# Transposing q and k on VectorE, with SBUF-to-SBUF moves, in place of TensorE transposes

## The chip, the cores and the metric

One Trainium2 chip (trn2), one core of it. The metric is the device time of one execution in microseconds (us), the median of the runs given. Times compared here are of fast runs. "The granted clock" is the share of full TensorE speed that the throttle granted, as the profile records it.

## The reference

Eight batches of strided sparse attention, whose output feeds a bilinear FFN. Four of the eight heads are *local* (each query sees the 32 positions up to itself), four are *strided* (it sees the earlier positions with the same remainder modulo 32).

```python
B, H, S, D = 8, 8, 576, 64
scores = (1/sqrt(D)) * q @ k.transpose(0, 1, 3, 2)
rel = pos[:, None] - pos[None, :]
mask_local   = (rel >= 0) & (rel < 32)                           # heads 0..3
mask_strided = (rel >= 0) & (pos[None, :] % 32 == pos[:, None] % 32)  # heads 4..7
attn_out = softmax(where(mask, scores, -1e9)) @ v
x = attn_out.transpose(0, 2, 1, 3).reshape(B * S, H * D)         # 4608 tokens x 512
out = ((x @ w_a) * (x @ w_b)) @ w_out                            # 512 -> 1536 -> 512
```

## The kernel before

The FFN runs in nine tiles of 512 tokens; each tile is 16 slots (12 of products with w_a and w_b, 4 of products with w_out). Batch 0's attention comes first; that of batch *b* is then woven into the slots of the tiles before it is needed. Its score matmuls on TensorE (PE) take q and k with the head dimension on the partitions; the program makes that layout with transposes on PE as well, and copies bring the result out of PSUM. `L` numbers in the profile lines are lines of the kernel file.

```python
def load_qk(b, strided):
    n, R, h0 = (NP, RS, HL) if strided else (96, RL, 0)
    for nm, src in (("q", q), ("k", k)):
        t = nat.tile([n, HL, R, D], BF16, tag=f"{nm}{R}", name=f"{nm}{R}")
        nc.gpsimd.dma_start(out=t, in_=src[b, h0:h0 + HL].rearrange("h (p r) d -> p h r d", r=R))
...
def step_T(b, c, nm):                       # transposes of one head pair on PE
    ...
        for g in range(8):                  # strided: 8 of 72 columns; local: 6 of 96
            nc.tensor.transpose(tv[:, g, :], sv[:, ...], ident[:NP, :NP])
    if nm == "k":
        nc.vector.tensor_copy(perm(kT_buf[b % 2][:, c, PAD:]), tv)
    else:                                   # each head's half of the rows, the rest stays zero
        for j in range(2):
            pr = slice(64 * j, 64 * j + 64)
            nc.scalar.copy(perm(qz_buf[b % 2][j][pr, c, :]), tv[pr])
...
def ffn_ab(t, f):
    ...                                     # 4 matmuls with w_a, 4 with w_b, into PSUM "mm" (3 buffers)
    nc.scalar.copy(a_sb, ab[0])
    nc.vector.tensor_mul(pf[:, f, :], a_sb, ab[1])      # called pf below
...
with tc.manual_schedule(engines={ENG.PE, ENG.SP, ENG.Pool}):   # in program order; VectorE's and
    ...                                                        # ScalarE's order is the compiler's
```

The softmax here doesn't subtract the row's maximum and nothing guards it: scores larger than these inputs give would overflow.

## Time and profile before

| | before |
|---|---|
| median of 3 runs | 365.77 us (364.46 to 365.85) |
| span of the profiled execution | 364.4 us |
| PE busy / granted clock | 343.3 us (94%), 2785 matmuls / 1.00 |
| VectorE (DVE) busy | 188.1 us (52%) |
| first FFN matmul | 29.5 us |
| the nine tiles | 46.4, 38.1, 37.0, 37.0, 37.0, 37.0, 36.5, 31.1, 34.8 us |

The last row is how the whole text reads time: a tile's length is the distance from its first w_a matmul to that of the next tile (to the span's end for the last). Here PE is the bound (94% busy, 91% of the chain that ended last), so a tile that is longer than its PE work has a wait in it. The profile's lines are shown in the prediction below.

### The profile page before, as it was taken

What the parts mean: (1) busy time and instruction counts of PE and PEld (TensorE: products, weight loads), DVE (VectorE), ACT (ScalarE), POOL (GpSimd) and SP (SyncE); (2) the same over time, 40 slices, a digit from 0 to 9 for tenths busy, and PEclk for the clock granted to TensorE, in tenths of its full rate; (3) what the DMA queues carried; (4) which work ended last, traced back from release to release, by engine and by line L of the source; (5) the groups of instructions that cost most, each with busy time, mean ns of one, the idle gap of its engine ahead of it and who ended that gap; (6) DMA issues with size and microseconds to landing.
All of it is one profiled execution on the core that took longest, in us unless ns stands there. A gap on an engine that the chain in (4) does not pass through costs nothing.

```text
span 364.4 us, 6796 instructions
## 1 busy us (share of the span) xinstructions
PE 343.3 (94%) x2785; PEld 185.5 (51%) x2785; DVE 188.1 (52%) x369; ACT 163.3 (45%) x268; POOL 90.8 (25%) x108
## 2 busy tenths in 40 slices
PE   1778898899999999999999999999999999999996
PEld 1563454555555554555455545554555544444443
DVE  6652467357643774377438643865276614313421
ACT  1662574357634762466237623663266313312321
POOL 8754648315310441044104410300000000000000
PEclk9999999999999999999999999999999999999999
DMA  9999999944892499649943995021402040011002
GB/s 105 132 201 188 184 200 170 196 91 67 63 108 86 67 110 130 149 63 101 143 148 45 109 143 159 0 67 34 144 6 65 26 141 19 0 58 59 0 28 89
DMA packets 88979, 35.47 MB, mean 97 GB/s; under 512 B 64588, under 2 KB 84108, under 8 KB 88948
## 3 DMA queue, kind: packets, MB, share of 16 engines
q0 software_dynamic: 68400, 19.69, 54.5%
q1 hardware_dynamic: 20548, 15.34, 15.9%
q8 instruction: 22, 0.36, 0.4%
q14 instruction: 9, 0.07, 0.1%
HBM read 39.31 MB, written 12.39 MB: 142 GB/s over the span
## 4 chain that ended last, share of the span: by engine, by line
PE 91%; ACT 3%; DVE 2%; DMA 1%; issue 1%; POOL 0%; DVEq 0%; POOLq 0%
PE mm L315 51%; PE mm L329 26%; PE st L227 5%; PE o L253 4%; PE tp L195 2%; ACT qz L203 2%; PE tp L185 2%; DMA k<-in_k_dram 1%; DVE xn L264 1%; ACT p L230 1%; DVE p L236 1%; PE tp L275 1%; PE mm L275 0%; PE tp L188 0%; DVE pf L320 0%
## 5 line engine op out<-in xcount | busy, mean ns | idle before, releaser
L320 DVE TENSOR_TENSOR pf<-a_sb,mm 128x512 bf16<-128x512 f32 x108 | 74.2, 687 | 82.2 <-PE mm L315 55.7
L315 PE MATMUL mm<-xT,wa_sb 128*128 128x512 bf16 x432 | 112.8, 384 | 0.0
L315 PE MATMUL mm<-xT,wb_sb 128*128 128x512 bf16 x432 | 111.8, 381 | 0.0
L329 PE MATMUL mm<-wo_sb,pf 128*128 128x512 bf16 (+1 forms) x444 | 96.4, 373 | 0.0
L319 ACT COPY a_sb<-mm 128x512 f32<-128x512 f32 x108 | 63.3, 586 | 60.6 <-PE mm L315 58.7
L315 PEld LDWEIGHTS <-wb_sb 128*128 128x128 bf16 x432 | 42.5, 98 | 51.9 <-issue 1.6
L329 PEld LDWEIGHTS <-pf 128*128 128x128 bf16 x444 | 42.3, 98 | 46.1
L315 PEld LDWEIGHTS <-wa_sb 128*128 128x128 bf16 x432 | 37.6, 99 | 33.0 <-issue 1.7
L230 ACT ACTIVATE p<-st 128x576 bf16<-128x576 f32 (+1 forms) x64 | 41.5, 649 | 26.3 <-PE st L227 25.0
L203 ACT COPY qz<-tp 64x576 bf16<-64x576 bf16 x56 | 35.4, 632 | 26.1 <-PE tp L185 13.1
L333 ACT COPY y_sb<-mm 128x512 f32<-128x512 f32 (+1 forms) x19 | 10.9, 575 | 66.4 <-PE mm L329 66.4
L264 DVE TENSOR_TENSOR xn<-o,rc 96x384 bf16<-96x384 f32 (+1 forms) x64 | 39.6, 619 | 1.9
L335 DVE COPY y_sb<-mm 128x512 f32<-128x512 f32 (+1 forms) x18 | 12.2, 677 | 54.5 <-PE mm L329 54.5
L227 PE MATMUL st<-qz,kT 128*72 128x72 bf16 (+1 forms) x448 | 30.0, 210 | 5.0 <-ACT qz L203 3.1
L157 POOL DMA_DIRECT2D vs<-in_v_dram x32 | 25.9, 813 | 32.5 <-PE o L253 21.5
L227 PEld LDWEIGHTS <-kT 128*72 128x72 bf16 (+1 forms) x448 | 25.4, 114 | 12.5 <-issue 5.6
L253 PEld LDWEIGHTS <-p 72*128 72x128 bf16 (+1 forms) x448 | 22.5, 101 | 17.7 <-DVE xn L264 6.5
L141 POOL COPY qp<-q 96x1536 bf16<-96x1536 bf16 x6 | 8.8, 1468 | 62.6 <-PE tp L185 62.6
L199 DVE COPY kT<-tp 128x576 bf16<-128x576 bf16 x28 | 16.6, 592 | 12.8 <-PE tp L185 11.0
L236 DVE TENSOR_TENSOR p<-p,mask_l 128x576 int16<-128x576 int16 x32 | 19.3, 604 | 3.7 <-ACT p L230 3.7
L236 DVE TENSOR_TENSOR p<-p,mask_s 72x576 int16<-72x576 int16 x32 | 16.7, 521 | 5.4 <-ACT p L230 5.3
L153 POOL DMA_DIRECT2D vl<-in_v_dram x8 | 11.7, 1457 | 19.0 <-PE st L227 18.0
(56 smaller groups left out, 169.7 us busy)
## 6 DMA issues: line engine op xcount, KB each, us to landing
out_dram<-y_sb SPq DMA_DIRECT2D x35, 256.0 KB, 2.4
q<-in_q_dram POOLq DMA_DIRECT2D x16, 288.0 KB, 5.7
k<-in_k_dram POOLq DMA_DIRECT2D x16, 288.0 KB, 7.1
xd<-xn SPq DMA_DIRECT2D x10, 288.0 KB, 3.2
vl<-in_v_dram POOLq DMA_DIRECT2D x7, 384.0 KB, 7.7
vs<-in_v_dram POOLq DMA_DIRECT2D x32, 72.0 KB, 7.7
wa_sb<-in_moe_w_a_dram POOLq DMA_DIRECT2D x4, 384.0 KB, 9.2
wb_sb<-in_moe_w_b_dram POOLq DMA_DIRECT2D x4, 384.0 KB, 9.8
```

Of the source, the lines that this page charges most:

```text
L157: nc.gpsimd.dma_start(out=vs_buf[b % 2][:, h, :, 0:D], in_=v[b, HL + h].rearrange("(p r) d -> p r d", r=RS))
L199: nc.vector.tensor_copy(perm(kT_buf[b % 2][:, c, PAD:]), tv)
L203: nc.scalar.copy(perm(qz_buf[b % 2][j][pr, c, :]), tv[pr])
L227: nc.tensor.matmul(st[:M, j, i * n:(i + 1) * n], lhsT=kT[:, c, k0:k0 + M], rhs=qz[j][:, c, q0:q0 + n], start=True, stop=True)
L230: nc.scalar.activation(p[:M, :, :W], st[:M, :, :W], ACT.Exp, scale=scale)
L236: nc.vector.tensor_tensor(pi, pi, mk, op=ALU.bitwise_and)
L253: nc.tensor.matmul(of[:, j, i, :], lhsT=p[:M, j, i * n:i * n + 128], rhs=vt, start=True, stop=True)
L264: nc.vector.tensor_mul(dst, ov[:, :, :, 0:D], rc[:n, :, :G].unsqueeze(3).to_broadcast([n, 2, G, D]))
L315: nc.tensor.matmul(ps_, lhsT=w[:, f // FC, kk, 128 * (f % FC):128 * (f % FC + 1)], rhs=xT[:, kk, TTOK * t:TTOK * (t + 1)], start=(kk == 0) ...
L319: nc.scalar.copy(a_sb, ab[0])
L320: nc.vector.tensor_mul(pf[:, f, :], a_sb, ab[1])
L329: nc.tensor.matmul(y, lhsT=pf[:, f, 128 * j:128 * (j + 1)], rhs=wo_sb[:, f, n * z:n * (z + 1)], start=(f == 0), stop=(f == FD - 1))
```

## The change

The intent is to take the q and k transposes off PE, the bound. From batch 1 on, loads bring q and k with 32 groups of 18 (local) or 24 (strided) neighbouring positions per head onto the partitions (of the strided groups 24 are the head's own, the other 8 read on past it and are padding); VectorE transposes them, laid out by the program as 32x32 blocks, into a block tile; DMAs issued by SyncE (SP), 24 per batch, move the blocks to where the score matmuls want them. GpSimd's reordering copies and the output's way through DRAM go. Batch 0, still through PE, scores on half arrays and so needs one copy of q instead of two. The diff, cut to its core:

```diff
 def load_qk(b, strided):
+    elif strided:
+        t = nat_s[b % 2][z]
+        tf = t.rearrange("p i d -> p (i d)")
+        if b < B - 1:
+            nc.gpsimd.dma_start(out=tf, in_=bass.AP(tensor=src.tensor, offset=(b * H + HL) * S * D,
+                                                    ap=[[S * D, HL], [YS * D, 32], [1, YS * D]]))
+        else:                       # last batch: one load per head of its 24 groups
+            for h in range(HL):
+                nc.gpsimd.dma_start(out=tf[32 * h:32 * h + YS], in_=src[b, HL + h].rearrange("(y i) d -> y (i d)", i=YS))
...
+def blocks(nm, z):
+    return sb.tile([128, 2, (S, RS * GP)[z]], BF16, tag=f"t{nm}{z}", name=f"t{nm}{z}", bufs=1)
+
+def step_D(b, z, nm, part):
+    if z == 0:                      # local, 2 parts of 576 elements
+        nc.vector.transpose(t.rearrange("p h (y i) -> p i h y", i=YL)[:, i],
+                            src[:, i].rearrange("p i (h d) -> p i h d", h=2))
+    else:                           # strided, 3 parts of 512 elements
+        nc.vector.transpose(t.rearrange("p h (r y i) -> p i r h y", r=RS, i=3)[:, part],
+                            src[:, RS * part:RS * (part + 1)].rearrange("p i (h d) -> p i h d", h=2))
+    if last:                        # 4 transfers for k, 8 for q
+        ... nc.sync.dma_start(out=kT_buf[...], in_=t[64 * c:64 * c + 64, e])
+        ... nc.sync.dma_start(out=qz_buf[...], in_=t[r0:r0 + 32, e])
...
-    def step_W(b, z): ...           # attention output through DRAM, batches 3 to 7
...
+        for z, nm, part, g in ((0, "k", 0, 3), (0, "k", 1, 5), (0, "q", 0, 7), (0, "q", 1, 9), (1, "k", 0, 11), ...
+                               (1, "q", 2, 15)):
+            do(g0 + g, step_D, b, z, nm, part)       # g0 = 16 * (b - 2): the slot that writes it
+    ... batch 1: step_D in slots 0 to 5
```

In the profiles `ql`, `kl` and `natq`, `natk` are q and k as loaded (local and strided), `tq` and `tk` the block tiles, `qz` and `kT` what the score matmuls read, `xn` the attention output divided by its sums.

More of the change, by code (lines that the diff above doesn't have):

```diff
@@ L18 @@
 NP = 72
-FIRST_W = 3
+GP = 96
+YL = 18
+YS = 24
 LW = 96
@@ L67, with qk_buf @@
     ident = const.tile([128, 128], BF16)
-    qz_buf = [[const.tile([128, KD, S], BF16, name=f"qz{i}{j}") for j in range(2)] for i in range(2)]
+    def qk_buf(nm):
+        return (const.tile([128, 2, S], BF16, name=f"{nm}l"), const.tile([128, 2, RS * GP], BF16, name=f"{nm}s"))
+    qz_buf = [[qk_buf(f"qz{i}{j}") for j in range(2)] for i in range(2)]
+    kT_buf = [(const.tile([128, 2, PAD + S], BF16, name=f"kT{i}l"), const.tile([128, 2, RS * GP + 32], BF16, name=f"kT{i}s"))
+              for i in range(2)]
+    nat_s = [[const.tile([128, YS, D], BF16, name=f"nat{nm}{i}") for nm in "qk"] for i in range(2)]
     vl_buf = [const.tile([128, HL * 6, VW], BF16, name=f"vl{i}") for i in range(2)]
@@ L74 @@
     mask_l = const.tile([128, 4, LW], I16)
-    kT_buf = [const.tile([128, KD, PAD + S], BF16, name=f"kT{i}") for i in range(2)]
     mask_s = const.tile([NP, NP], I16)
@@ L89, in consts @@
                 nc.vector.memset(p[:, :, W:], 0.0)
-        nc.vector.memset(kT_buf[i][:, 0:2, 0:PAD], 0.0)
+        nc.vector.memset(kT_buf[i][0][:, :, 0:PAD], 0.0)
+        nc.vector.memset(kT_buf[i][1], 0.0)
         for j in range(2):
-            nc.vector.memset(qz_buf[i][j][64 * (1 - j):64 * (2 - j)], 0.0)
+            for t in qz_buf[i][j]:
+                nc.vector.memset(t, 0.0)
         nc.vector.memset(vl_buf[i][:, :, D:D + 1], 1.0)
@@ L128, in load_qk @@
     def load_qk(b, strided):
-        n, R, h0 = (NP, RS, HL) if strided else (96, RL, 0)
-        for nm, src in (("q", q), ("k", k)):
-            t = nat.tile([n, HL, R, D], BF16, tag=f"{nm}{R}", name=f"{nm}{R}")
-            nc.gpsimd.dma_start(out=t, in_=src[b, h0:h0 + HL].rearrange("h (p r) d -> p h r d", r=R))
-            nats[b, nm, strided] = t
-    perm_t = {}
-    def perm_qk(b):
-        for nm in ("q", "k"):
-            t = nat.tile([96, RL, HL, D], BF16, tag=f"{nm}p", name=f"{nm}p", bufs=1)
-            nc.gpsimd.tensor_copy(t.rearrange("p r h d -> p h r d"), nats[b, nm, False])
-            perm_t[b, nm] = t
+        if b == 0:
+            n, R, h0 = (NP, RS, HL) if strided else (96, RL, 0)
+        for z, (nm, src) in enumerate((("q", q), ("k", k))):
+            if b == 0:
+                t = nat.tile([n, HL, R, D], BF16, tag=f"{nm}{R}", name=f"{nm}{R}", bufs=1)
+                nc.gpsimd.dma_start(out=t, in_=src[b, h0:h0 + HL].rearrange("h (p r) d -> p h r d", r=R))
+            elif strided:
[6 more added lines that the diff above has]
+                    for h in range(HL):
+                        nc.gpsimd.dma_start(out=tf[32 * h:32 * h + YS],
+                                            in_=src[b, HL + h].rearrange("(y i) d -> y (i d)", i=YS))
+            else:
+                t = nat.tile([128, YL, D], BF16, tag=f"{nm}l", name=f"{nm}l", bufs=1)
+                nc.gpsimd.dma_start(out=t.rearrange("p i d -> p (i d)"),
+                                    in_=src[b, 0:HL].rearrange("h (y i) d -> (h y) (i d)", i=YL))
+            nats[b, nm, strided] = t
     def load_vl(b):
@@ L170, in load_wo @@
         )
+    tl = {}
+    def blocks(nm, z):
+        return sb.tile([128, 2, (S, RS * GP)[z]], BF16, tag=f"t{nm}{z}", name=f"t{nm}{z}", bufs=1)
     def step_T(b, c, nm):
         src = nats[b, nm, c >= 2]
-        if b == 0:
-            tp = pmm.tile([128, S], BF16, tag="mm", name="mm")
-        else:
-            tp = ptp.tile([128, S], BF16, tag="tp", name="tp")
+        tp = pmm.tile([128, S], BF16, tag="mm", name="mm")
         if c < 2:
@@ L183, in step_T @@
             for r in range(RL):
-                if b > 1:
-                    nc.tensor.transpose(tv[:, r, :], perm_t[b, nm][:, r, 2 * c:2 * c + 2, :], ident[:96, :96])
-                    continue
                 for hh in range(2):
@@ L195, in step_T @@
                 nc.tensor.transpose(tv[:, g, :], sv[:, 2 * (c - 2) + g // 4, g % 4, :], ident[:NP, :NP])
-            perm = lambda t: t
-            tv = tp
+            perm = lambda t: t.rearrange("d (g p) -> d g p", p=GP)[:, :, :NP]
         if nm == "k":
-            nc.vector.tensor_copy(perm(kT_buf[b % 2][:, c, PAD:]), tv)
-        else:
-            for j in range(2):
-                pr = slice(64 * j, 64 * j + 64)
-                nc.scalar.copy(perm(qz_buf[b % 2][j][pr, c, :]), tv[pr])
+            t = kT_buf[0][c // 2][:, c % 2]
+            nc.vector.tensor_copy(perm(t[:, PAD:] if c < 2 else t[:, :RS * GP]), tv)
+        else:
+            if c % 2 == 0:
+                tl[b, c // 2, nm] = blocks("q", c // 2)
+            nc.scalar.copy(perm(tl[b, c // 2, nm][:, c % 2]), tv)
+    def step_D(b, z, nm, part):
+        src = nats[b, nm, z == 1]
+        if part == 0:
+            tl[b, z, nm] = blocks(nm, z)
+        t = tl[b, z, nm]
+        if z == 0:
+            i = slice(YL // 2 * part, YL // 2 * (part + 1))
+            nc.vector.transpose(t.rearrange("p h (y i) -> p i h y", i=YL)[:, i],
+                                src[:, i].rearrange("p i (h d) -> p i h d", h=2))
+            last = part == 1
+        else:
+            nc.vector.transpose(t.rearrange("p h (r y i) -> p i r h y", r=RS, i=3)[:, part],
+                                src[:, RS * part:RS * (part + 1)].rearrange("p i (h d) -> p i h d", h=2))
+            last = part == 2
+        if last:
+            for c in range(2):
+                for e in range(2):
+                    if nm == "k":
+                        dst = kT_buf[b % 2][z][64 * e:64 * e + 64, c]
+                        nc.sync.dma_start(out=dst[:, PAD:] if z == 0 else dst[:, :RS * GP], in_=t[64 * c:64 * c + 64, e])
+                        continue
+                    for j in range(2):
+                        r0 = 64 * c + 32 * j
+                        nc.sync.dma_start(out=qz_buf[b % 2][j][z][64 * e + 32 * j:64 * e + 32 * j + 32, c],
+                                          in_=t[r0:r0 + 32, e])
     def step_Tk(b, c):
@@ L213, in unit @@
         c, half = u // 2, u % 2
-        M, n, G = (128, LW, 3) if c < 2 else (NP, NP, 4)
-        segs = [(G * half + i) * n for i in range(G)]
-        return c, half, M, n, G, segs
+        return (c, half, 128, LW, 3) if c < 2 else (c, half, NP, NP, 4)
     ps = {}
     def step_S(b, u):
-        c, half, M, n, G, segs = unit(u)
-        kT, qz = kT_buf[b % 2], qz_buf[b % 2]
+        c, half, M, n, G = unit(u)
+        kT = kT_buf[b % 2][c // 2]
+        qz = [tl[0, c // 2, "q"]] * 2 if b == 0 else [x[c // 2] for x in qz_buf[b % 2]]
         st = pst.tile([128, 2, 512], F32, tag="st", name="st")
-        for i, q0 in enumerate(segs):
-            k0 = q0 + (0 if c < 2 else PAD)
+        for i in range(G):
+            k0 = (G * half + i) * (LW if c < 2 else GP)
             for j in range(2):
-                nc.tensor.matmul(st[:M, j, i * n:(i + 1) * n], lhsT=kT[:, c, k0:k0 + M],
-                                 rhs=qz[j][:, c, q0:q0 + n], start=True, stop=True)
+                d = slice(64 * j, 64 * j + 64) if b == 0 else slice(0, 128)
+                nc.tensor.matmul(st[:, j, i * n:(i + 1) * n], lhsT=kT[d, c % 2, k0:k0 + 128],
+                                 rhs=qz[j][d, c % 2, k0:k0 + n], start=True, stop=True)
         p = p_buf[(B * b + u) % 3]
@@ L241, in step_V @@
     def step_V(b, u):
-        c, half, M, n, G, segs = unit(u)
+        c, half, M, n, G = unit(u)
         p = ps.pop((b, u))
@@ L250, in step_V @@
                     vt = vl_buf[b % 2][:, (2 * c + j) * 6 + 3 * half + i, 0:D + 1]
+                elif b == 0:
+                    vt = vs_buf[b % 2][:, 2 * (c - 2) + half, 2 * i + j, 0:D + 1]
                 else:
-                    vt = vs_buf[b % 2][:, 2 * (c - 2) + half, 2 * i + j, 0:D + 1]
+                    vt = vs_buf[b % 2][:, 2 * (c - 2) + j, 4 * half + i, 0:D + 1]
                 nc.tensor.matmul(of[:, j, i, :], lhsT=p[:M, j, i * n:i * n + 128], rhs=vt,
@@ L259, in step_V @@
         x = xn[b, c // 2][:, :, 2 * (c % 2):2 * (c % 2) + 2, :]
-        if c < 2:
-            dst = x[:, 3 * half:3 * half + 3].rearrange("p g j d -> p j g d")
+        if c < 2 or b:
+            dst = x[:, G * half:G * half + G].rearrange("p g j d -> p j g d")
         else:
@@ L281, in step_X @@
         nc.scalar.copy(dst, tv)
-    def step_W(b, z):
-        xd = dram.tile([S, 4 * D], BF16, tag=f"xd{z}", name=f"xd{z}")
-        x = xn[b, z].rearrange("p g h d -> p g (h d)")
-        if z == 0:
-            nc.sync.dma_start(out=xd.rearrange("(g p) e -> p g e", p=LW), in_=x)
-        else:
-            nc.sync.dma_start(out=xd.rearrange("(p g) e -> p g e", g=RS), in_=x)
-        nc.sync.dma_start_transpose(out=xT[:, 2 * z:2 * z + 2, S * b:S * (b + 1)], in_=xd)
-    SEQ_X = (("Tk0",), ("Tq0",), ("S0", "Tk1"), ("S1", "Tq1"), ("V0", "S2"), ("V1", "S3", "Tk2"), ("V2", "Tq2"),
-             ("V3", "S4", "X0"), ("S5", "Tk3"), ("V4", "X1"), ("V5", "Tq3"), ("S6",), ("S7", "X2"), ("V6",),
-             ("V7",), ("X3",))
-    SEQ_W = (("Tk0",), ("Tq0",), ("S0", "Tk1"), ("S1", "Tq1"), ("V0", "S2"), ("V1", "S3", "Tk2"), ("V2", "Tq2"),
-             ("V3", "S4", "W0"), ("S5", "Tk3"), ("V4", "Tq3"), ("V5", "S6"), ("S7",), ("V6",), ("V7", "W1"))
-    FN = {"Tk": step_Tk, "Tq": step_Tq, "S": step_S, "V": step_V, "X": step_X, "W": step_W}
+    DENSE = (("S0",), ("S1",), ("V0", "S2"), ("V1", "S3"), ("V2", "X0", "S4"), ("V3", "S5"), ("V4", "X1", "S6"),
+             ("V5", "S7"), ("V6", "X2"), ("V7",), ("X3",))
+    SEQ = (("S0",), ("S1",), ("V0",), ("S2",), ("V1",), ("S3", "X0"), ("V2",), ("S4",), ("V3",), ("S5", "X1"),
+           ("V4",), ("S6",), ("V5",), ("S7", "X2"), ("V6",), ("V7",), ("X3",))
+    FN = {"Tk": step_Tk, "Tq": step_Tq, "S": step_S, "V": step_V, "X": step_X}
     def run(b, slot):
@@ L371, with do @@
             slots += [(ffn_ab, t, f) for f in range(FD)] + [(ffn_y, t, j) for j in range(4)]
-        todo = []
-        for b in range(1, B):
-            todo.append((b, 2 if b == 1 else 16 * (b - 1) - 2, list(SEQ_X if b < FIRST_W else SEQ_W)))
-        loads = {}
+        todo = [(b, 3 if b == 1 else 16 * (b - 1) - 2, list(DENSE if b == 1 else SEQ)) for b in range(1, B)]
+        at = {}
+        def do(i, fn, *args):
+            at.setdefault(i, []).append(lambda: fn(*args))
         for b in range(2, B):
             g0 = 16 * (b - 2)
-            loads[g0 + 1] = lambda b=b: load_qk(b, False)
-            loads[g0 + 5] = lambda b=b: load_vl(b)
-            loads[g0 + 8] = lambda b=b: load_qk(b, True)
-            loads[g0 + 11] = lambda b=b: (load_vs(b), perm_qk(b))
+            do(max(g0 - 2, 0), load_qk, b, False)
+            do(g0 + 3, load_qk, b, True)
+            do(g0 + 6, load_vl, b)
+            do(g0 + 10, load_vs, b)
+            for z, nm, part, g in ((0, "k", 0, 3), (0, "k", 1, 5), (0, "q", 0, 7), (0, "q", 1, 9), (1, "k", 0, 11),
+                                   (1, "k", 1, 12), (1, "k", 2, 12), (1, "q", 0, 13), (1, "q", 1, 14),
+                                   (1, "q", 2, 15)):
+                do(g0 + g, step_D, b, z, nm, part)
+        for z, nm, part, g in ((0, "k", 0, 0), (0, "k", 1, 0), (0, "q", 0, 1), (0, "q", 1, 1), (1, "k", 0, 2),
+                               (1, "k", 1, 3), (1, "k", 2, 3), (1, "q", 0, 4), (1, "q", 1, 5), (1, "q", 2, 5)):
+            do(g, step_D, 1, z, nm, part)
         for i, (fn, t, j) in enumerate(slots):
             fn(t, j)
-            if i in loads:
-                loads[i]()
+            for f in at.get(i, ()):
+                f()
             for b, g0, seq in todo:
@@ L388 @@
                     run(b, seq.pop(0))
-                    if b == 1 and i in (3, 12):
-                        run(b, seq.pop(0))
 _INS = ['q', 'k', 'v', 'moe_w_a', 'moe_w_b', 'moe_w_out']
```

## The prediction

> **What bounds the kernel now.** I read the page's engine shares first, then the chain of work that ended last.
>
> ```profile
> PE 343.3 (94%) x2785; PEld 185.5 (51%) x2785; DVE 188.1 (52%) x369; ACT 163.3 (45%) x268; POOL 90.8 (25%) x108
> PE   1778898899999999999999999999999999999996
> DMA  9999999944892499649943995021402040011002
> ...
> PE 91%; ACT 3%; DVE 2%; DMA 1%; issue 1%; POOL 0%; DVEq 0%; POOLq 0%
> ```
>
> TensorE (PE) is busy in nearly every slice and is 91% of the chain; VectorE (DVE) and ScalarE (ACT) are half idle. The exception is the start: the first eight slices (0 to 73 us) show full DMA engines and a PE with holes. So a microsecond of PE work removed in the later stages is a microsecond gained; early on, loads may take its place. To see whether PE also waits inside its busy time I cut the span at the starts of the first matmul of each 512-token FFN tile:
>
> ```profile
> core 0: us, PE busy (x) PEld busy (x) DVE busy (x) ACT busy (x) POOL busy (x), PEclk, DMA share, GB/s
> 0.00:29.46 29.46, 15.65 (x221) 13.46 (x222) 17.45 (x47) 13.12 (x20) 21.40 (x34) 1.00 1.32 147
> 29.46:75.90 46.44, 42.66 (x380) 22.48 (x378) 23.67 (x43) 21.16 (x35) 24.06 (x28) 1.00 1.57 188
> 75.90:113.96 38.06, 38.06 (x345) 20.99 (x342) 21.08 (x42) 20.57 (x34) 10.56 (x11) 1.00 0.60 79
> 113.96:150.97 37.01, 37.01 (x316) 19.96 (x314) 21.60 (x42) 18.33 (x30) 10.57 (x11) 1.00 0.98 107
> ...
> 298.68:329.76 31.08, 31.08 (x146) 14.09 (x144) 9.64 (x14) 8.20 (x14) 0.00 (x0) 1.00 0.09 34
> ```
>
> A tile without attention takes 31.08 us; with batch 2 beside it 38.06, with batches 3 to 7 37.01. From 75.9 us on PE is busy all the time: attention simply adds its own matmul time, 7.0 us (batch 2) or 5.9 us (later ones). The timeline of PE gives the price of each piece as the distance between starts:
>
> ```profile
> 48.49 0.42 PE L227 MATMUL st<-qz,kT 128*128 128x96 bf16 x6
> 48.75 0.43 PE L195 MATMUL tp<-ident,k 72*128 72x72 bf16 x8
> 49.01 1.03 PE L315 MATMUL mm<-xT,wa_sb 128*128 128x512 bf16 x4
> 49.88 1.03 PE L315 MATMUL mm<-xT,wb_sb 128*128 128x512 bf16 x4
> ```
>
> Eight 72-column transposes: 49.01 - 48.75 = 0.26 us, 32.5 ns each. Six 96-column matmuls: 0.26 us, 43 ns each. Four of 512 columns: 0.87 us, 216 ns each. Cost follows columns, so rows of the weights don't matter: padding the strided score weights from 72 to 128 columns should cost nothing.
>
> [...]the first 24 FFN matmuls are one piece of 7.64 us in the chain, against 24 x 0.216 = 5.18[...]. [...]a k load that lands in 4.9 us alone takes 15.2 us among the weight loads.
>
> **The change, part by part.** *PE, removed.* The transposes of q and k for batches 1 to 7: 224 of 72 columns x 32.5 ns = 7.3 us; 144 of 96 columns (batches 2 to 7) x 42.5 ns = 6.1 us; batch 1's 48 half-width ones, four groups of 12 at 0.38 us = 1.5 us, and about 0.1 us each on the FFN group behind (8 matmuls in 1.83 instead of 1.73), 0.4. Sum 15.3 us. *PE, added.* The output transposes come back for batches 3 to 7, which had used a DMA through DRAM: per batch 12 x 42.5 + 16 x 32.5 ns = 1.03 us, times five 5.2 us. Check: batch 2's tile (which has them) less batch 3's, 38.06 - 37.01 = 1.05. Net -10.1 us: 2785 matmuls become 2785 - 416 + 140 = 2509. Per tile: about 36.0 us from batch 2 on.
>
> *DVE.* Ten transposes per batch, 4 of 576 and 6 of 512 elements[...], so 7.4 us per batch, 52 us in all. Gone: 28 copies of kT (16.6 us). Zeroing padded buffers whole adds some 2.3 us. Per 36 us tile DVE goes from 21.6 to about 26 us, 73%. In the slots of FFN work that hold a transpose it does 0.69 (pf) + 0.45 (mask) + 0.78 = 1.9 us in about 2.0 to 2.2 us of PE time: tight, but beside it. *ACT.* q copies of batches 1 to 7 go (35.4 us), 20 xT copies come (12.6 us). It stays far from the bound. *GpSimd.* The reordering copies go. They held up DVE:
>
> ```profile
> 56.27 1.48 POOL L141 COPY qp<-q 96x1536 bf16<-96x1536 bf16 x1
> 57.68 1.47 POOL L141 COPY kp<-k 96x1536 bf16<-96x1536 bf16 x1
> ...
> 56.61 2.85 DVE L236 TENSOR_TENSOR p<-p,mask_s 72x576 int16<-72x576 int16 x1
> ```
>
> The mask takes 2.85 us instead of 0.45 and ends just as the GpSimd copies do. In later batches nothing waits for it, but here PE then stands 0.93 us for a value and 0.94 us for the next exp.
>
> *DMA.* 24 SBUF-to-SBUF transfers per batch move 2 x 0.29 + 2 x 0.39 = 1.38 MB; the four DRAM transfers that disappear moved 1.18 MB. Five to six slots lie between the last transpose and the scores that need it, 10 us or more, against 2 to 4 us for a transfer in the quiet stages: hidden.
>
> *Batch 0.* Scores on half arrays need one q copy in place of two, so ACT loses 0.64 us from the chain before the scores of each of four head pairs. ACT is not the only wait there (GpSimd's masks, the 0.7 us DVE divisions, now more memsets), so of 2.6 us I take 1.5.
>
> *Batch 1's tile* took 46.44 us. Its work is 31.08 + 2.5[...] + about 7.7 of attention = 41.3, so 5.2 us are stalls. I expect those from the GpSimd copies (1.9 us) and from the q copies on ACT (1.2 us) to vanish. But loads become nearer: the last wo chunk landed at 53.4 us, for use at 61.5. With the prologue and the transposes shortened PE would want it at about 55, while batch 1's transfers (1.38 MB) and a third more bytes in the strided loads push it to 56 or 58. And batch 2's k landed at 56.4 us; its transpose sits in the order of DVE. So I give all 3 us back to new waits.
>
> Sum: 365.8 - 10.1 - 1.5 - 3 + 3 = **354 us**, 3.2% less.
>
> **Rivals.** (a) *DVE waits at the head of its queue for loads.* DVE takes its work in order; a transpose of batch 2 placed before its data lands holds the pf multiplications behind it, and with three PSUM buffers PE stops within a slot or two. The program's positions (slots 3 to 9) are some 40 to 52 us, the landing 56 to 60 us. For: the DMA row is full until 73 us, and batch 1's strided k landed at 40.0 us, when slot 3 already runs. Against: the order on DVE is not the program's (at 49.29 us a kT copy runs ahead of the xn product written before it), so the compiler may place them later. It would cost 5 to 18 us once: 359 to 370. (b) *DVE becomes the bound of the steady tiles*, if a transpose takes 1.5 us instead of 0.75: then 33 to 34 of 36 us, and the half-filled slots overflow by about 0.7 us five times per tile, six tiles: +15 to 20 us, near 372.[...] (c) *Nothing new waits, and batch 1's stalls go*: 354 - 3 = 351, or 349 with the whole of batch 0's 2.6 us. (d) *Transfers late, scores wait*: 1 us per batch would make 360. Against: ten us of slack.
>
> **Range and chances.** The -10.1 us rests on counted instructions and is safe if PE remains the bound. The start is uncertain, mostly to the worse side: (c) sets the low end at 347.5, a moderate (a) the high end at 363. The 2% line is 358.5 us, 4.5 above my number; (a), (b) and (d) together cross it some 3 times in 10, beyond +2% only in the bad forms of (a) or (b). Chances: faster 0.70, same 0.22, slower 0.08.
>
> **What would show it.** Right: 2509 matmuls; tiles from the second on of 36.0 us with PE busy throughout; transposes of 0.7 to 0.8 us; DVE busy 210 to 225 us, ACT about 138 us; no 2.85 us mask; the first FFN matmul at about 28 us. Wrong: DVE rows with idle time ended by a q or k load between 35 and 65 us and PE waiting for pf behind them (rival a); transposes above 1.2 us, or PE gaps in the late tiles ended by DVE (b); score matmuls waiting for DMA (d); a first tile that still takes 46 us because wo lands late would make the right total only by luck.

The 42.5 ns for 96 columns: the starts in such groups lie mostly 42 or 43 ns apart in the trace of the kernel before, and with the 43 of the timeline above the sum moves by less than 0.1 us. The 0.78 and 0.71 us of a transpose, which make the 7.4 us per batch (4 x 0.78 + 6 x 0.71): no trace at the time had one; the first experiment below measured both, for one way of writing. The 2.5 us in batch 1's tile: 7.64 - 5.18, of which nearly all is in the first 12 FFN matmuls, which start some 0.42 us apart (29.46 to 34.54 us), the next 12 some 0.22; the clock record of that profile begins at 34.5 us. For rival (a)'s order of DVE, with pf held up and PE out of PSUM buffers, the changed kernel gives the numbers: DVE idle for 9.85 us ahead of a transpose with pf behind it, PE for 8.61 (below).

## The result, and the profile after

The changed kernel takes **467.5 us** (465.72 to 470.22, 4 runs) against 365.63 us (4 runs) of the kernel before in the same rounds: ratio 1.280 (1.272 to 1.288). A ratio here and below is the mean time of one kernel's fast runs over the mean of the other's fast runs of the same rounds, so it is not quite the ratio of the medians that are quoted. The result compares equal to the reference.

The page of the changed kernel: engine totals, granted clock in tenths per fortieth of the span, shares of the chain that ended last, and the q and k loads (count, size, median us from issue to landing).

```profile
PE 357.0 (76%) x2509; PEld 181.7 (39%) x2509; DVE 271.4 (58%) x417; ACT 136.2 (29%) x228; POOL 73.6 (16%) x102
...
PEclk9999795889977997759977799879999999999999
...
PE 52%; DMA 25%; DVE 12%; issue 6%; SPq 3%; POOL 1%; DVEq 0%; ACT 0%; POOLq 0%
...
natq<-in_q_dram POOLq DMA_DIRECT2D x6, 384.0 KB, 18.8
natk<-in_k_dram POOLq DMA_DIRECT2D x6, 384.0 KB, 18.7
ql<-in_q_dram POOLq DMA_DIRECT2D x7, 288.0 KB, 6.1
kl<-in_k_dram POOLq DMA_DIRECT2D x7, 288.0 KB, 7.5
```

The matmul count is as predicted, and yet the chain is only 52% PE. A quarter of it is transfers. The strided loads (natq, natk) take 18.8 us where the local ones take 6 to 7.5, for a third more bytes. DVE is busy 271 us, not 210 to 225. PE's own busy time has not fallen by 10 us but risen by 14 (357.0 for 343.3): in the stages where it waits, the granted clock is lower (0.82 in tiles 0 and 2, below, against 1.00 before), off and on through the first two thirds of the span, and the mean w_a matmul takes 415 ns for 384.

Where the time is, by tiles:

| us | first FFN | tile 0 | 1 | 2 | 3 | 4 | 5 | 6 | 7 | 8 |
|---|---|---|---|---|---|---|---|---|---|---|
| before | 29.5 | 46.4 | 38.1 | 37.0 | 37.0 | 37.0 | 37.0 | 36.5 | 31.1 | 34.8 |
| after | 41.5 | 75.8 | 51.4 | 56.7 | 55.5 | 48.6 | 37.8 | 35.4 | 31.1 | 34.5 |

Of the 104 us of difference between the spans, 12 are before the FFN, 29 in tile 0 and 63 in tiles 1 to 4: this is not a disturbance of the start alone. Tile 0 and tile 2 by the windows of the trace (length, busy time of PE, PEld, DVE, ACT, POOL with counts, granted clock, DMA share, GB/s):

```profile
41.50:117.30 75.80, 46.65 (x301) 22.44 (x299) 48.39 (x59) 17.03 (x28) 20.05 (x26) 0.82 1.55 136
168.70:225.30 56.60, 41.16 (x288) 20.49 (x285) 33.22 (x49) 15.46 (x26) 7.25 (x9) 0.82 0.56 79
```

Tile 2 holds the steady mix, with DVE busy 33 of 57 us and PE 41: *no* engine is full. Something makes them wait in turn. The transposes, by form (count, busy us and mean ns, then idle time of DVE just ahead of them and what ended it):

```profile
L231 DVE STREAM_TRANSPOSE tq<-ql 128x576 bf16<-128x576 bf16 x14 | 36.5, 2607 | 8.4 <-DMA ql<-in_q_dram 8.4
L231 DVE STREAM_TRANSPOSE tk<-kl 128x576 bf16<-128x576 bf16 x14 | 36.4, 2625 | 0.6 <-DMA kl<-in_k_dram 0.6
L235 DVE STREAM_TRANSPOSE tq<-natq 128x512 bf16<-128x512 bf16 x21 | 20.4, 1010 | 42.2 <-DMA kT1l<-tk 17.0 <-DMA kT0l<-tk 13.2 <-DMA natq<-in_q_dram 8.3
L235 DVE STREAM_TRANSPOSE tk<-natk 128x512 bf16<-128x512 bf16 x21 | 19.3, 1005 | 9.4 <-DMA kT0s<-tk 4.7 <-DMA vs<-in_v_dram 2.9 <-DMA kT1s<-tk 1.8
```

The local ones take 2.6 us, the strided ones 1.0, together 112.6 us where 52 were predicted; and DVE stands idle for 42.2 us ahead of the strided q transposes. One such wait, in the timeline of DVE in tile 2, and what PE does meanwhile (start, length, in brackets the idle time before):

```profile
175.38 0.55 DVE L312 TENSOR_TENSOR xn<-o,rc 96x384 bf16<-96x384 f32 x1
185.78 1.03 DVE L235 STREAM_TRANSPOSE tq<-natq 128x512 bf16<-128x512 bf16 x1 [9.85 <-DMA kT0l<-tk]
```
```profile
187.39 1.01 PE L352 MATMUL mm<-xT,wa_sb 128*128 128x512 bf16 x2 [8.61 <-DVE pf L357]
```

This transpose stands in DVE's queue three pf into tile 2. The program writes it in the last slots of the tile, after the twelfth; the compiler, which orders DVE, put it there. Its own load is not what it waits for: it belongs to batch 4, whose natq was issued at 112.06 and landed at 128.60 us. It waits for the block tile tq, which has one buffer and is still being read by eight transfers of the batch before, the last of which landed at 185.66 (the semaphores that it waits for are those of the eight; kT0l in the brackets is a name that the profile infers from the semaphore, and kT0l's own transfers landed only from 186.02 us on). These moves took 6.5 to 12.7 us each, beside the slow loads of the batch after: natq was in flight from 165.86 to 185.12, natk from 166.57 to 185.84 us. Behind the transpose stands the next pf, so PE runs out of PSUM buffers and waits 8.6 us.

So there are three suspects, not one: transposes that are too long, loads that are too slow, and an order that makes DVE wait for what the loads hold up.

### The profile page after: what moved, and what is told of

The parts are those of the page before. It is cut to its first block, busy times and chain, and to the rows that moved or that the text cites. A ratio compares the mean times of both kernels' runs of the same rounds, so it can differ in the third digit from the quotient of the medians.

```text
span 468.2 us, 6489 instructions
## 1 busy us (share of the span) xinstructions
PE 357.0 (76%) x2509; PEld 181.7 (39%) x2509; DVE 271.4 (58%) x417; ACT 136.2 (29%) x228; POOL 73.6 (16%) x102
## 4 chain that ended last, share of the span: by engine, by line
PE 52%; DMA 25%; DVE 12%; issue 6%; SPq 3%; POOL 1%; DVEq 0%; ACT 0%; POOLq 0%
PE mm L352 29%; PE mm L366 18%; DMA natk<-in_k_dram 6%; DMA qz11s<-tq 4%; DMA kl<-in_k_dram 4%; DVE tq L231 3%; DVE tk L231 3%; DMA qz01s<-tq 2%; SPq L247 2%; PE o L301 2%; DMA kT0l<-tk 2%; PE st L273 2%; DMA qz00s<-tq 2%; DVE pf L357 2%; DMA wa_sb<-in_moe_w_a_dram 2%
## 5 line engine op out<-in xcount | busy, mean ns | idle before, releaser
L352 PE MATMUL mm<-xT,wa_sb 128*128 128x512 bf16 x432 | 124.5, 415 | 32.9 <-DVE pf L357 32.7
L352 PE MATMUL mm<-xT,wb_sb 128*128 128x512 bf16 x432 | 120.5, 405 | 0.0
L352 PEld LDWEIGHTS <-wa_sb 128*128 128x128 bf16 x432 | 40.7, 105 | 71.8 <-issue 43.7
L235 DVE STREAM_TRANSPOSE tq<-natq 128x512 bf16<-128x512 bf16 x21 | 20.4, 1010 | 42.2 <-DMA kT1l<-tk 17.0
L312 DVE TENSOR_TENSOR xn<-o,rc 96x384 bf16<-96x384 f32 (+1 forms) x64 | 42.1, 657 | 1.6
L231 DVE STREAM_TRANSPOSE tq<-ql 128x576 bf16<-128x576 bf16 x14 | 36.5, 2607 | 8.4 <-DMA ql<-in_q_dram 8.4
L231 DVE STREAM_TRANSPOSE tk<-kl 128x576 bf16<-128x576 bf16 x14 | 36.4, 2625 | 0.6 <-DMA kl<-in_k_dram 0.6
L323 PE MATMUL tp<-ident,xn 72*128 72x72 bf16 (+1 forms) x196 | 13.6, 208 | 26.0 <-DVE xn L312 26.0
L301 PE MATMUL o<-vs,p 72*128 72x65 bf16 x256 | 14.6, 204 | 21.6 <-DVE xn L312 21.6
L329 ACT COPY xT<-tp 128x576 bf16<-128x576 bf16 x28 | 17.8, 635 | 39.4 <-PE tp L323 39.4
L235 DVE STREAM_TRANSPOSE tk<-natk 128x512 bf16<-128x512 bf16 x21 | 19.3, 1005 | 9.4 <-DMA kT0s<-tk 4.7
## 6 DMA issues: line engine op xcount, KB each, us to landing
natq<-in_q_dram POOLq DMA_DIRECT2D x6, 384.0 KB, 18.8
natk<-in_k_dram POOLq DMA_DIRECT2D x6, 384.0 KB, 18.7
```

Of the source, the lines that this page charges most:

```text
L231: nc.vector.transpose(t.rearrange("p h (y i) -> p i h y", i=YL)[:, i], src[:, i].rearrange("p i (h d) -> p i h d", h=2))
L235: nc.vector.transpose(t.rearrange("p h (r y i) -> p i r h y", r=RS, i=3)[:, part], src[:, RS * part:RS * (part + 1)].rearrange("p i (h d) ...
L301: nc.tensor.matmul(of[:, j, i, :], lhsT=p[:M, j, i * n:i * n + 128], rhs=vt, start=True, stop=True)
L312: nc.vector.tensor_mul(dst, ov[:, :, :, 0:D], rc[:n, :, :G].unsqueeze(3).to_broadcast([n, 2, G, D]))
L323: nc.tensor.transpose(tv[:, g, :], x[:, g].rearrange("p j d -> p (j d)"), ident[:n, :n])
L329: nc.scalar.copy(dst, tv)
```

## The experiments

Ten kernels ran. The factorial core is eight kernels: each of three repairs alone, each pair, all three, and none. "Loads" splits the strided load by head, "dense" makes the transposes write neighbouring elements, "order" takes DVE's order from the program. Dense kernels other than the last one below score on permuted columns, so they are wrong. The comparison with the reference does not notice: the scores are so small that the softmax is nearly uniform. Their shapes, counts and bytes are those of the change.

### The cost of a transpose by its write step

```diff
 # the kernel before, with transposes added behind its last eviction, nothing else changed
+        for s, g in ((1, 9), (2, 9), (3, 3), (4, 3), (6, 3), (8, 3), (9, 1), (16, 1), (18, 1)):
+            d = xdst[:, 0:g * 64 * s].rearrange("p (g x i) -> p g i x", x=64, i=s)[:, :, 0:9 // g]
+            nc.vector.transpose(d, xsrc.rearrange("p (g i) d -> p g i d", g=g))
+        ...  # and the 512-element form of the change, once with write step 3, once with step 1
```

> The kernel before, with eleven VectorE transposes appended behind its last eviction, which read one 128x576 tile and write it with steps of 1, 2, 3, 4, 6, 8, 9, 16 and 18 elements between neighbours (the changed kernel writes 18 in the local heads, 3 in the strided ones), and two of 512 elements in the forms of the strided heads, with step 3 and with step 1. Theory 'write step': 0.75 to 0.8 us at step 1, 1.0 to 1.1 at step 3, 2.6 at 18, rising between. Rival 'the local form is slow for another reason' (more elements, the source's shape, GpSimd at work beside it in the changed kernel): all steps cost about the same here, either all near 0.8 us or all near 2.6.

One look (382.74 us, state unknown); only the durations of the added instructions count. Same engine, same source, same number of elements; only the distance between neighbouring elements written differs. The timeline shows, in order, 576 elements at steps 1, 3, 6 and 18, and then the 512-element form at steps 3 and 1:

```profile
361.07 0.78 DVE L314 STREAM_TRANSPOSE xdst<-xsrc 128x576 bf16<-128x576 bf16 x1
...
362.73 1.13 DVE L314 STREAM_TRANSPOSE xdst<-xsrc 128x576 bf16<-128x576 bf16 x1
...
365.39 2.09 DVE L314 STREAM_TRANSPOSE xdst<-xsrc 128x576 bf16<-128x576 bf16 x1
...
375.62 2.64 DVE L314 STREAM_TRANSPOSE xdst<-xsrc 128x576 bf16<-128x576 bf16 x1
378.30 1.02 DVE L316 STREAM_TRANSPOSE xdst<-xsrc 128x512 bf16<-128x512 bf16 x1
379.35 0.71 DVE L318 STREAM_TRANSPOSE xdst<-xsrc 128x512 bf16<-128x512 bf16 x1
```

All nine, in ns: step 1: 778, 2: 820, 3: 1129, 4: 1454, 6: 2092, 8: 2726, 9: 2702, 16: 2580, 18: 2639. The prediction's 0.78 and 0.71 us are what step 1 takes. Step 2 adds 42 ns, step 3 351 and step 4 676; beyond step 8 the time no longer grows (2580 to 2726 ns). The run shows the curve alone, not its mechanism.

### The strided load split by head

```diff
-                nc.gpsimd.dma_start(out=tf, in_=bass.AP(tensor=src.tensor, offset=(b * H + HL) * S * D,
-                                                        ap=[[S * D, HL], [YS * D, 32], [1, YS * D]]))
+                for h, w in ((h, (b * H + HL + h) * S * D) for h in range(HL)):
+                    nc.gpsimd.dma_start(out=tf[32 * h:32 * h + 32],
+                                        in_=bass.AP(tensor=src.tensor, offset=w, ap=[[YS * D, 32], [1, YS * D]]))
```

> The changed kernel with each load of strided q or k split into one transfer per head of 32 rows (four instead of one), so that the outermost dimension of the source is 32 and not 4. Theory 'loads': the one transfer [...]lands in 18 to 27 us, holds VectorE at the head of its queue and is most of the loss; then the loads land in 5 to 15 us and the total falls from 467 to 410 or less. Theory 'transposes': the 2.6 us of each local transpose (28 of them, 73 us instead of 22) are most of the loss; then the total stays above 440.

447.42 us (447.25 to 450.73), ratio 1.225 (1.2205 to 1.2294). Each of the four loads lands 7.7 (q) and 6.4 us (k) after its issue, median; all four, the bytes of the one load before, have landed 10.1 and 9.6 us after the first issue, in place of 18.8 and 18.7. The idle time ahead of the strided q transposes falls from 42.2 to 14.5 us, and the moves that held tq take 3.4 to 7.3 us in tile 2. The traffic differs too: while the two whole loads were the only ones on GpSimd's queue (173 to 180 us in the changed kernel), its packets took 39.4% of the time of 16 engines; while two loads of the kernel before were alone (123.3 to 125.9 us), 110% by the same count. Which engines took part the trace doesn't show. Other transfers landed later beside the slow loads: the fourth wa chunk landed at 55.1 us in the changed kernel, at 43.8 before and at 46.6 with the loads split; the last wo chunk at 66.2, 53.4 and 56.8; and the moves took up to 12.7 us in tile 2, where about 2 us is usual in quiet stages (medians of 1.9 to 2.2 us between 295 and 375 us, one group at 3.4).

This run is not quite a pure test: with more loads the compiler ordered DVE somewhat differently. The pairs below, in program order, are.

### Transposes that write neighbouring elements

```diff
-            nc.vector.transpose(t.rearrange("p h (y i) -> p i h y", i=YL)[:, i],
+            nc.vector.transpose(t.rearrange("p h (i y) -> p i h y", i=YL)[:, i],
...
-            nc.vector.transpose(t.rearrange("p h (r y i) -> p i r h y", r=RS, i=3)[:, part],
+            nc.vector.transpose(t.rearrange("p h (r i y) -> p i r h y", r=RS, i=3)[:, part],
```

> The changed kernel with every VectorE transpose writing its 32 columns next to each other (result wrong on purpose: the columns are in another order); all instructions of all engines keep their order, loads are unchanged. Theory 'transposes': they take about 0.75 us, VectorE falls from 271 to about 205 us busy, and the total falls below 420. Theory 'loads': the transposes get short as well, but VectorE waits for the strided loads instead, and the total stays above 440.

427.49 us (422.01 to 430.12), ratio 1.163 (1.1554 to 1.1713); the ratio uses fast runs (their median is 427.11). The order of instructions on every engine is identical to that of the change, so the 40 us are due to the write step alone. But the idle time ahead of the strided q transposes did not move: 42.3 us here, 42.2 in the change. In this run shorter transposes did not shorten the wait for the moves.

### Both

```diff
+ for h, w in ((h, (b * H + HL + h) * S * D) for h in range(HL)): ...   # the loads as above
+ t.rearrange("p h (i y) -> p i h y", i=YL) ...                         # the transposes as above
```

> Both edits (result wrong on purpose). If these two are the whole loss, the prediction's sum holds: 350 to 362 us, tiles of 36 us from the second on. If a third cost is there (24 transfers a batch at 0.6 us of issue each on the sync queue, their landing among the loads, or VectorE's fixed order), the total stays above 370.

399.21 us (395.66 to 400.76), ratio 1.088 (1.082 to 1.0937). The transposes by form:

```profile
L235 DVE STREAM_TRANSPOSE tq<-natq 128x512 bf16<-128x512 bf16 x21 | 14.0, 690 | 13.2 <-DMA kT0l<-tk 7.3 <-DMA kT1l<-tk 5.5 <-issue 0.4
...
L231 DVE STREAM_TRANSPOSE tq<-ql 128x576 bf16<-128x576 bf16 x14 | 10.3, 750 | 13.5 <-DMA ql<-in_q_dram 10.1 <-DMA qz11l<-tq 2.4 <-DMA qz00l<-tq 0.9
```

Durations are now those of the prediction, the idle time ahead of the strided q transposes fell from 42 to 13 us, and still the kernel is 33 us slower than before. Tiles 2 to 4 are 40.6, 40.6 and 39.9 us where 36.0 were predicted. What remains in them, in the timeline of DVE and then of PE:

```profile
147.37 0.55 DVE L312 TENSOR_TENSOR xn<-o,rc 96x384 bf16<-96x384 f32 x1
151.50 0.71 DVE L235 STREAM_TRANSPOSE tq<-natq 128x512 bf16<-128x512 bf16 x1 [3.58 <-DMA kT0l<-tk]
```
```profile
152.84 1.17 PE L352 MATMUL mm<-xT,wa_sb 128*128 128x512 bf16 x4 [2.07 <-DVE pf L357]
```

It is the wait of the changed kernel, shorter: the transpose three pf into the tile waits for the single block tile, whose last transfer of the batch before landed at 151.38 us. Both instructions were legal where the compiler put them; the place is nine pf, three quarters of a tile, ahead of the program's.

### And DVE in program order

```diff
-    with tc.manual_schedule(engines={ENG.PE, ENG.SP, ENG.Pool}):
+    with tc.manual_schedule(engines={ENG.PE, ENG.SP, ENG.Pool, ENG.DVE}):
```

> Both edits of the run before (dense writes, loads per head; result wrong on purpose) and VectorE's instructions kept in the order of the program, as TensorE's are, instead of the compiler's order. Theory 'order': the compiler hoists transposes to where it believes their inputs ready; on the chip they wait there for loads, and for the single block buffer whose 8 transfers have not been issued, and hold pf behind them. Then the first FFN matmul comes at about 28 us instead of 35.4, tiles 2 to 4 (counted from 0) fall from 40.6 to 36.0 us; the first tile stays long (60 us or more), since the program itself has batch 2's transposes in slots 3 to 9 and their data lands at about 60 us. Total 370 to 385. Rival 'issue': the sync queue, at 0.6 us for each of 24 transfers a batch, is the limit; then those tiles stay at 40 us.

378.67 us (377.02 to 379.2), ratio 1.034 (1.0312 to 1.0367). A steady tile by its window (columns as above):

```profile
96.50:132.40 35.90, 35.90 (x288) 18.87 (x286) 24.89 (x49) 15.29 (x26) 9.74 (x15) 1.00 0.75 121
```

PE is busy for all of 35.90 us at full clock; the prediction had 36.0. The steady stage is repaired, and the kernel gains there what was promised. Nearly all that is left is in tile 0, 65.6 us against 46.4 before. Its largest wait on DVE:

```profile
59.27 0.78 DVE L231 STREAM_TRANSPOSE tk<-kl 128x576 bf16<-128x576 bf16 x1 [18.92 <-DMA kl<-in_k_dram]
```

That is rival (a) of the prediction as it was written: batch 2's k, wanted in slot 3, was issued at 43.29 and landed at 59.19 us among the weights.

### Program order in the change itself, and the missing pairs

```diff
-    with tc.manual_schedule(engines={ENG.PE, ENG.SP, ENG.Pool}):        # the changed kernel, nothing else
+    with tc.manual_schedule(engines={ENG.PE, ENG.SP, ENG.Pool, ENG.DVE}):
```

> The changed kernel with nothing but the order of VectorE changed to the program's. If the order alone is the main cost, below 410 us. If slow transposes[...] are costs of their own, it stays above 430: transposes of 2.6 us in slots of 2 us, loads of 18 us that are issued some 8 slots (16 us) before use.

424.9 us (423.59 to 428.08), ratio 1.162 (1.1572 to 1.1674). The first FFN matmul comes at 31.2 us in place of 41.5, and tiles 1 to 4 take 44.2, 44.9, 41.3 and 44.2 in place of 51.4, 56.7, 55.5 and 48.6 us. Tile 0 gets no shorter (77.9 for 75.8): there the program's own order waits for loads.

```diff
+    engines={..., ENG.DVE}, and "p h (i y) -> p i h y": order and dense; the load of four heads stays
```

> The changed kernel with dense writes and the program's order[...] (result wrong on purpose). With the other corners of the three-way table this gives the cost of the loads alone, against e4_order (378.7). The loads are issued some 8 slots, 16 us, before use and take 18 us: if they matter in the steady tiles too, those take 38 to 42 us and the total is 395 to 415; if only in the crowded start, tiles stay at 36 and the total is below 392.

402.99 us (401.43 to 406.1), ratio 1.100 (1.0967 to 1.1033). Its tiles 1 to 4 are 40.6 to 41.8 us although DVE's order is the program's: DVE now waits 6.24 us for a buffer of the output y_sb, still being stored, while natq (130.22 to 148.71 us) and natk are under way; that they hold up the store is inferred from this overlap. Tile 5, beside which only the last batch's per-head loads remain, is 35.9.

```diff
+    engines={..., ENG.DVE}, and one strided load per head: order and loads; "p h (y i) -> p i h y" stays
```

> The changed kernel with loads per head and the program's order, but the transposes of 2.6 and 1.0 us (right result). Against e4_order (378.7) this gives the cost of the write step alone. In the slots with a local transpose VectorE has 0.69 + 0.45 + 2.6 = 3.7 us of work against 2.2 of TensorE: 1.5 us over, four times a tile, so tiles of about 41 us from batch 2 on, +5 us each in five or six tiles, and the total 405 to 415. If the excess is absorbed by the idle slots around it, tiles stay below 38 and the total below 392.

397.43 us (396.49 to 398.23), ratio 1.087 (1.0838 to 1.0899). A steady tile by its window, then one of its transposes on DVE, and the wait of PE that follows when the mask, pf and xn written behind it come late:

```profile
178.80:217.70 38.90, 36.31 (x289) 18.99 (x287) 32.94 (x49) 15.57 (x26) 9.77 (x15) 1.00 0.72 116
```
```profile
191.98 2.64 DVE L231 STREAM_TRANSPOSE tk<-kl 128x576 bf16<-128x576 bf16 x1
```
```profile
196.24 0.30 PE L323 MATMUL tp<-ident,xn 96*128 96x96 bf16 x3 [1.23 <-DVE xn L312]
```

Each of tiles 1 to 5 is 38.9 us, 3.0 above 35.9: short waits of PE behind DVE, at full clock, with DVE 33 of 39 us busy.

All eight, medians in us (the kernel before lay between 365.63 and 365.98 in all the rounds that they come from):

| | slow loads | loads split |
|---|---|---|
| compiler's order, step 18 and 3 | 467.5 (the change) | 447.4 |
| compiler's order, dense | 427.5 | 399.2 |
| program order, step 18 and 3 | 424.9 | 397.4 |
| program order, dense | 403.0 | 378.7 |

Reading it pair by pair: splitting the loads saves 20.1 to 28.3 us whatever the rest is. Dense transposes save 40.0 and 48.2 in the compiler's order, but 21.9 and 18.7 in the program's; program order saves 42.6 and 50.0 with long transposes, 24.5 and 20.5 with dense ones. The last two overlap by some 20 to 30 us: a long transpose costs about double in the compiler's order. So each of the three is real, none alone explains the result, and the shares don't add up to a sum. Of the expectations, that of "loads" alone put 447 us on the side of the transposes; "dense" and "order" alone fell between their two totals, so neither of the single-cause theories held; "order and loads" fell between its two as well (397 us and tiles of 38.9 us, where 405 to 415 and about 41 had been expected); and with all three the first FFN matmul came at 30.9 us, not at 28.

### Batch 1's and 2's transposes later

```diff
-        todo = [(b, 3 if b == 1 else 16 * (b - 1) - 2, list(DENSE if b == 1 else SEQ)) for b in range(1, B)]
+        todo = [(b, 5 if b == 1 else 19 if b == 2 else 16 * (b - 1) - 2, list(DENSE if b < 3 else SEQ)) for b in range(1, B)]
-                do(g0 + g, step_D, b, z, nm, part)
+                do(g0 + g if b > 2 else 14 + z * 2 + (nm == "q"), step_D, b, z, nm, part)
... batch 1's strided transposes in slots 5 to 7 instead of 2 to 5
```

> e4_order with the transposes of batches 1 and 2 moved to slots in which their loads have landed (batch 1's strided heads in slots 5 to 7, batch 2 in slots 14 to 17), and the attention of batch 1 started at slot 5, of batch 2 at slot 19. If early loads are what is left, the first tile falls from 60 to about 48 us and the total to 355 to 365, near the prediction. If the serial issue of transfers is in the way, score matmuls of batches 1 and 2 wait for transfers by 5 us or more each and the total stays above 365.

On top of all three repairs: 369.76 us (367.95 to 372.01), ratio 1.009 (1.0033 to 1.0151). Tile 0 fell from 65.6 to 52.9 us and tile 1, which now holds batch 2's attention at double pace, rose from 35.9 to 41.2: of the 12.7 us that the early transposes cost, 5.3 came back as new work and waits one tile on. What now ends waits, in the chain in order of time (start, length):

```profile
42.17 1.06 SPq L247
43.28 4.92 DMA qz11l<-tq
...
58.51 6.26 DMA qz11s<-tq
```

SP needs some 0.6 us for each of the 24 transfers of a batch, one after the other (588 ns in the median for the q moves of the changed kernel; 589 to 1063 for four of them here, between 35 and 60 us), and in the crowded start the last one lands 5 to 6 us later (4.92 and 6.26 above). PE's scores wait 4.30 and 4.17 us for them.

### Batches 0 and 1 through TensorE, the rest through VectorE

```diff
+FB = 2
-        if b == 0:                                   # in load_qk, step_S, step_V
+        if b < FB:
+                        nc.gpsimd.dma_start(out=tf[32 * h:32 * h + 32], in_=bass.AP(       # strided, per head
+                            tensor=src.tensor, offset=o, ap=[[RS * D, 32], [32 * RS * D, 3], [1, RS * D]]))
+                    nc.gpsimd.dma_start(out=t[32 * h:32 * h + 32], in_=bass.AP(            # local, per head
+                        tensor=src.tensor, offset=(b * H + h) * S * D, ap=[[D, 32], [32 * D, YL], [1, D]]))
+    do(4, zero_q, 0)                                 # zeroing of padded q buffers moved out of the start
+    do(8, zero_q, 1)
... batch 2 transposed in slots 12 to 15 and scored from slot 18; DVE in program order; dense transposes
```

> A repaired version with right results: batches 0 and 1 by TensorE with scores on half arrays, batches 2 to 7 by VectorE with writes of step 1 (the loads bring positions 32 apart into one partition's rows, so that the 32 columns of a block are neighbours), loads per head, VectorE in the order of the program, batch 2 transposed in slots 12 to 15 and scored from slot 18, zeroing of q's buffers moved into the FFN. If the four costs found so far are all there is: first FFN matmul at 28 to 30 us, first tile about 44, second 36 to 39, then 35.9 each; total 354 to 358, 2 to 3% faster than before. If transfers between SBUF partitions still make scores wait, the second tile is above 40 and the total about 360 or more.

**356.6 us** (356.23 to 357.09), ratio 0.975 (0.9732 to 0.9775): 2.5% faster than the kernel before. The load now puts position 32i + y on row y (in the strided heads the group of eight positions with that number), so that the dense transpose writes position order; the result is right by construction, not only by the comparison (which, as said, would pass a permuted one). The page (engine totals, clock, chain), the strided q transposes by form, and a steady window:

```profile
PE 334.5 (94%) x2589; PEld 174.3 (49%) x2589; DVE 209.1 (59%) x411; ACT 138.1 (39%) x232; POOL 114.7 (32%) x170
...
PE 90%; DVE 4%; ACT 2%; DMA 2%; issue 1%; POOL 0%; DVEq 0%; POOLq 0%
```
```profile
L245 DVE STREAM_TRANSPOSE tq<-natq 128x512 bf16<-128x512 bf16 x18 | 12.3, 695 | 0.2 <-DMA out_dram<-y_sb 0.2
```
```profile
112.00:148.00 36.00, 36.00 (x287) 18.92 (x285) 24.98 (x50) 15.41 (x27) 14.12 (x22) 1.00 0.97 132
```

PE is the bound again: 90% of the chain, 42.2 us of idle time ahead of those transposes down to 0.2. Against before: first FFN matmul 28.0 instead of 29.5 us, tile 0 45.4 for 46.4, tile 1 37.4 for 38.1, tiles 2 to 5 35.9 for 37.0, tile 6 35.4 for 36.5, and 0.3 in the last: 9.0 us.

## Why the prediction was wrong

**The step that failed first** is the transposes' term: "*DVE.* Ten transposes per batch, 4 of 576 and 6 of 512 elements", taken at 0.78 and 0.71 us, "so 7.4 us per batch, 52 us in all." Counts were right; the durations hold for a dense write (0.78 and 0.71 us in the first experiment). The diff's write patterns have steps of 18 and 3 elements, and there they are 2.6 and 1.0 us: 28 x 2.62 + 42 x 1.01 = 113 us by the groups after. The step was in the diff and was not priced. I had even priced it as a rival: (b), 1.5 us for each, +15 to 20 us. Ten of 1.5 us are 15 us a batch; in the kernel they are 4 x 2.62 + 6 x 1.01 = 16.5. And the table shows 18.7 us for it, where nothing else is amiss (397.4 - 378.7). The rival's size was right.

**The second failed step** is "*DMA.* ... hidden", with the loads entering only as "a third more bytes in the strided loads". The bytes were right and not what counted: landing took 18.8 us, and 10.1 for the same bytes as one load per head; the last batch's loads in the same diff, already one per head, were a hint. The moves, taken at "2 to 4 us for a transfer in the quiet stages", took up to 12.7 beside these loads. Worth 20 to 28 us.

**The third** is rival (a), "once: 359 to 370". The mechanism was right in part: DVE is held at the head of its queue, with pf behind (9.85 us in tile 2). That it would come once, at the start, and for a load was wrong: in tile 2 it is held by a buffer that moves are still reading. I took the compiler's freedom on DVE's order as a point *against* it ("may place them later"). In tile 2 it placed the transposes three quarters of a tile earlier, in front of a single-buffered tile still being emptied. Worth 20 to 50 us, before the first FFN matmul and in tiles 1 to 4. In program order the rival's own version stands, in tile 0: 18.92 us of idle DVE.

**The fourth went along with these:** all sums were at full clock. The granted clock was 0.82 in tiles 0 and 2 of the changed kernel, where PE waited up to 11.4 and 8.6 us at a time, and 1.00 in the same tiles of the kernel before (its record begins at 34.5 us), and PE busy time rose by 14 us with 276 matmuls fewer. The prediction counted such a loss once, the 2.5 us at the first FFN matmuls. Here the stages with long waits lost more than the waits' own length (in tile 2 PE was busy for 41.2 us with 288 matmuls, before for 37.0 with 316); those with waits of 1.2 to 1.4 us, order and loads repaired, did not: the clock in that run's steady tile was 1.00. That the waits lower the clock is inferred from these windows.

**What was right.** 2509 matmuls; ScalarE 136.2 us for "about 138"; no long mask (2.85 us before, at most 0.64 after); steady tiles of 35.9 us for 36.0 once nothing waits, so that the net -10.1 us of PE work is real (from tile 2 on 1.1 us a tile, as worked out) and padding the weights from 72 to 128 columns is free (a group of 8 strided score matmuls takes 0.28 us of the chain before, 0.26 after). Batch 0's -1.5 us came in the mixed kernel (28.0 for 29.5), where the zeroing of the q buffers was moved away and batch 1 went through PE; with all three repairs alone it did not (30.9). Which of the two did it was not tried. One sum of the prediction slips without effect: rival (c)'s 349 is 351 - 1.1 = 350.

**The chances.** "Slower" got 0.08, because (a), (b) and (d) were each priced alone, and given 3 chances in 10 together to cross the 2% line. All three happened: (d) too, as 4.3 us waits of scores for transfers once the rest was mended. They share a cause, that loads, transposes and moves form one chain through DVE's queue, so that what delays one delays the next; weighing them one by one hid that.

**What stays open.** Why a write step costs what it does (the curve is measured, the mechanism not). On how many DMA engines the four-head load ran (the packets of two such loads took 39.4% of the time of 16). Whether a second buffer for the block tile would have mended the order's cost as well: no run tried it. In the mixed kernel's tile 0, 45.4 us against the 41.3 of work that the prediction counted, PE is busy for 42.1; the other 3.3 us are waits of at most 1.0 us each, which nobody pursued. How the overlap of write step and order divides between the wait itself and the clock.

## What to carry to other kernels

Before pricing an operation moved to another engine, read both access patterns in the diff: the step of the innermost written dimension on VectorE, and how each load is cut (here one over four heads, or one per head), since these made an operation here 3.4 and 1.9 times as long for the same bytes (2.62 us for 0.78, 18.8 for 10.1). Where the compiler sets an engine's order, look up in the trace where it put an instruction: here it was three quarters of a tile ahead of the program, and work that depends on a late transfer, ahead of work that the bound engine needs, did better in program order and behind the landing. Here work taken off the bound paid in the steady stage only; in the start, full of loads, the old path was the better one (356.6 against 369.8 us, though these two kernels differ in more than that).
